# Loading the last row block of an output projection early, through the software DMA queue, in a decode-layer kernel

## The chip, the cores and the metric

The kernel runs on one core of a Trainium2 chip. The metric is device time in microseconds (us). Each run lists the time, the span of the core (first to last instruction that the profile shows) and the mean clock that the throttle granted to the matrix engine (1.0 is full speed).

Names used below: PE is the matrix engine (PEld its weight loads), DVE the vector engine, ACT the scalar engine, POOL the GpSimd engine, SP the engine that issues most transfers. The profile counts 16 DMA engines for a core. A "queue" is where an engine puts its transfers: SP's is q1, ACT's is q10, the software queue that GpSimd fills is q0, and q8 and q14 carry instruction fetches.

## The reference, cut to what matters

```python
# x [8,1,512]; k_cache, v_cache [8,8,4096,128]; wq [512,4096]; wo [4096,512]; bf16
xn = _layernorm(x, axis=-1)
s  = attention(xn, k_cache[..., -1024:, :], v_cache[..., -1024:, :], wq) @ wo   # 32 heads, 8 kv heads
g  = _silu((_gelu(xn @ w_gate) * (xn @ w_up)) @ w_down)                          # width 1792
return x + s * g
```

With 8 tokens, nearly everything is reading weights and cache: 47.6 MB for each execution.

## The kernel before

The kernel streams everything through one SP queue, in the order of use: wq, then keys and values in 1 MB pieces, then the three FFN matrices, then wo. Partition p of a wo tile holds wo rows p*32 to p*32+31. One of these 32 "outer rows" j is a 128 x 512 block of 128 KB: 1 KB on each partition. The output projection is 32 steps of two matmuls, one step for each j, in the order of arrival. The last loads are made smaller and smaller, so that little work is left when the last one lands.

```python
    nc.scalar.dma_start(out=x_sb, in_=x_flat)              # the early copy of x, for the layer norm
    # ... 16 groups of attention; then, with g == NGR, the last loads:
            parts = [(0, 16), (16, 24), (24, 28), (28, 30), (30, 31), (31, 32)]
            wo_t = [load_wo(*q) for q in parts[:2]]        # load_wo issues on nc.sync (the SP queue)
            for t in range(2):
                nc.sync.dma_start(
                    out=x_res[64 * t : 64 * t + B, :], in_=x_flat[:, t * 256 : (t + 1) * 256]
                )
            wo_t += [load_wo(*q) for q in parts[2:]]
    # ...
    for q, (j0, j1) in enumerate(parts):
        for j in range(j0, j1):
            for t in range(2):
                c0 = (j - j0) * D + t * 256
                nc.tensor.matmul(
                    s_ps[64 * t : 64 * t + 64, 0:256],
                    og[:, j : j + 2, :].rearrange("p m b -> p (m b)"),
                    wo_t[q][:, c0 : c0 + 256],
                    start=(j == 0), stop=(j == NOR - 1),
                    tile_position=(0, 64 * t), skip_group_check=True,
                )
    # then out = x_res + s_ps * g_sb on DVE, and two stores
```

The softmax here doesn't subtract the row's maximum and nothing guards it: scores larger than these inputs give would overflow.

## Time and profile before

| | before |
|---|---|
| time, median of 3 runs (range) | 120.79 us (120.64 to 120.92) |
| span of the profiled run | 119.1 us |
| moved by DMA | 47.61 MB, mean 400 GB/s |
| PE, DVE, ACT busy | 73%, 54%, 34% |
| last wo load complete | 115.60 us after the span's start |
| last matmul ends | 115.94 us |

These are lines of the profile page of the kernel before. The rows of digits cut the span into 40 slices of about 3 us; a digit is the busy share or the granted clock of a slice in tenths. The queue lines give packets, MB and the share of 16 engines' time. The last line gives a transfer's size in KB and the median us from issue to landing.

```profile
PE 86.8 (73%) x929; PEld 62.1 (52%) x929; DVE 64.2 (54%) x149; ACT 40.4 (34%) x78; POOL 4.2 (4%) x10
...
PEclk9999999555799999999999999999999965555999
DMA  4999999999999999999999999999999999999940
GB/s 88 432 396 440 418 426 432 418 432 424 418 432 432 432 402 435 429 418 426 429 426 421 429 424 421 429 426 424 429 424 442 426 424 448 420 440 402 405 165 3
...
q1 hardware_dynamic: 6240, 47.46, 95.0%
q8 instruction: 7, 0.11, 0.3%
...
slot<-in_A_k_cache_dram SPq DMA_DIRECT2D x16, 1024.0 KB, 19.7
```

The DMA row stands at 9 from the second slice to the 38th, at a rate that never leaves 396 to 448 GB/s, while no compute engine is that busy. A 1 MB load lands 19.7 us after its issue; such loads complete about 2.45 us apart, so I estimate that it stands in a full queue, about eight deep (19.7 / 2.45). The kernel is bound by its DMA engines.

The end of the chain of waits of the kernel before (start us, length us, what):

```profile
100.62 13.72 DMA slot<-in_A_wo_dram
114.34 0.04 issue
114.38 0.63 PE big L523 x8
...
115.98 0.44 DVE tmp L534
```

And the same place in its timeline (start us, busy us, engine, line, operation, tiles, count, and in brackets the idle time before and what ended it):

```profile
110.60 1.94 PE L523 MATMUL big<-wide_slot,og 128*64 128x256 bf16 x32 [1.60 <-DMA wide_slot<-in_A_wo_dram]
...
114.38 1.56 PE L523 MATMUL big<-slot,og 128*64 128x256 bf16 x16 [0.21 <-DMA slot<-in_A_wo_dram]
...
115.98 0.42 DVE L534 TENSOR_TENSOR tmp<-big,g_sb 128x256 bf16<-128x256 f32 x1 [2.19 <-PE big L523]
```

PE waits for each wo part and ends 0.34 us after the last has landed (115.60 to 115.94). What decides the time is when the last part is complete.

A load shows up to 16 landing events ("posts"), which I read as one from each engine that has a share in it: in this trace the loads of wo over 128 partitions have 16 each, and `x_sb`, in 8 rows, has 8. The load is complete at the last of them: PE's last two matmuls start 0.04 us after it (115.60 to 115.64). The 16 posts of the last part are not in the views above; I list them from the trace (us from the span's start):

```text
113.91 113.95 114.00 114.07 114.09 114.13 | 114.33 114.58 114.85 | 115.24 115.29 115.37 115.39 115.53 115.58 115.60
```

Six engines are done 1.5 us before the last; seven are 1.3 to 1.7 us late. That is the slack that the change is after.

### The profile page before, as it was taken

How to read it: one execution, taken by the hardware profiler on the slowest of the kernel's cores; microseconds unless marked ns; L12 is line 12 of the kernel's file. 1: busy time of each engine (PE TensorE's matmuls, PEld its weight loads, DVE VectorE, ACT ScalarE, POOL GpSimd, SP SyncE). 2: the span in 40 equal slices, each digit the busy share in tenths (PEclk: the TensorE clock that was granted, in tenths of full speed). 3: DMA queues.
4: the chain of work that ended last, by engine and by line, in shares of the span. 5: the costliest groups of instructions: out<-in, count | busy, mean ns of one | idle time of the engine just before them, and what ended most of it. 6: DMA issues, size and time to landing. Idle time of an engine off the chain costs nothing.

```text
span 119.1 us, 2281 instructions
## 1 busy us (share of the span) xinstructions
PE 86.8 (73%) x929; PEld 62.1 (52%) x929; DVE 64.2 (54%) x149; ACT 40.4 (34%) x78; POOL 4.2 (4%) x10
## 2 busy tenths in 40 slices
PE   0013946786999999999998797977979843546680
PEld 0003813563767777686775584755847630133650
DVE  5340644643666866876694664945748424622211
ACT  4000314792443562464354342453424403001100
POOL 7600000000000000000000000000000000000000
PEclk9999999555799999999999999999999965555999
DMA  4999999999999999999999999999999999999940
GB/s 88 432 396 440 418 426 432 418 432 424 418 432 432 432 402 435 429 418 426 429 426 421 429 424 421 429 426 424 429 424 442 426 424 448 420 440 402 405 165 3
DMA packets 6281, 47.61 MB, mean 400 GB/s; under 512 B 728, under 2 KB 1024, under 8 KB 1280
## 3 DMA queue, kind: packets, MB, share of 16 engines
q1 hardware_dynamic: 6240, 47.46, 95.0%
q8 instruction: 7, 0.11, 0.3%
q10 hardware_dynamic: 32, 0.01, 0.0%
q14 instruction: 2, 0.02, 0.0%
HBM read 47.46 MB, written 0.01 MB: 399 GB/s over the span
## 4 chain that ended last, share of the span: by engine, by line
DMA 57%; PE 24%; DVE 10%; ACT 2%; SPq 2%; issue 1%; DVEq 0%
DMA wide_slot<-in_B_w_gate_dram 18%; DMA slot<-in_A_v_cache_dram 16%; PE t_ps L244 12%; DMA slot<-in_A_wo_dram 12%; DMA wide_slot<-in_A_wq_dram 11%; DVE kT L250 8%; PE sc_ps L270 5%; PE o_ps L304 3%; PE big L411 1%; PE big L523 1%; DVE q_all L395 1%; ACT q_all L395 1%; PE big L366 1%; DVE q_sb L379 1%; ACT p L283 1%
## 5 line engine op out<-in xcount | busy, mean ns | idle before, releaser
L250 DVE COPY kT<-t_ps 128x1024 bf16<-128x1024 bf16 x48 | 31.8, 688 | 26.4 <-PE t_ps L244 24.5
L244 PE MATMUL t_ps<-ident_f,slot 128*128 128x128 f32 x256 | 38.5, 301 | 7.8 <-DMA slot<-in_A_k_cache_dram 7.8
L244 PEld LDWEIGHTS t_ps<-ident_f,slot 128*128 128x128 f32 x256 | 31.2, 154 | 18.0 <-issue 7.2
L250 ACT COPY kT<-t_ps 128x1024 bf16<-128x1024 bf16 x16 | 16.2, 1012 | 16.9 <-PE t_ps L244 16.5
L283 ACT ACTIVATE p<-sc_ps 128x512 bf16<-128x512 f32 x16 | 9.6, 597 | 28.4 <-PE sc_ps L270 28.4
L270 PE MATMUL sc_ps<-kT,q_all 128*32 128x512 bf16 x128 | 10.7, 405 | 3.9 <-ACT q_all L395 1.8
L291 DVE STREAM_TRANSPOSE pT<-p 128x512 bf16<-128x512 bf16 x16 | 11.2, 703 | 2.8 <-ACT p L283 2.8
L304 PE MATMUL o_ps<-slot,pT 128*32 128x256 bf16 x256 | 10.1, 278 | 0.0
L324 PE MATMUL a_ps<-selr,o_sb 128*128 128x16 f32 x64 | 9.6, 263 | 0.4 <-ACT o_sb L314 0.3
L324 PEld LDWEIGHTS a_ps<-selr,o_sb 128*128 128x128 f32 x64 | 8.4, 192 | 0.6 <-ACT o_sb L314 0.6
L270 PEld LDWEIGHTS <-q_all 128*32 128x32 bf16 x128 | 3.3, 95 | 7.9 <-issue 3.2
L304 PEld LDWEIGHTS <-pT 128*32 128x32 bf16 x256 | 5.5, 97 | 2.9 <-issue 2.5
L314 ACT COPY o_sb<-o_ps 128x256 f32<-128x256 f32 x16 | 6.0, 378 | 1.3 <-PE o_ps L304 1.3
L260 PE MATMUL sc_ps<-far,hot 4*128 4x512 bf16 x16 | 6.4, 398 | 0.0
L411 PE MATMUL big<-wide_slot,xT 128*32 128x448 bf16 x32 | 3.4, 571 | 3.8 <-DMA wide_slot<-in_B_w_up_dram 2.2
L523 PEld LDWEIGHTS <-og 128*64 128x64 bf16 x64 | 3.5, 109 | 3.7 <-DMA wide_slot<-in_A_wo_dram 2.1
L220 PE MATMUL t_ps<-ident,xhat 32*128 32x32 bf16 x4 | 0.3, 195 | 6.6 <-DVE xhat L210 6.6
L320 PEld LDWEIGHTS a_ps<-ss,ones_f 128*128 128x128 f32 x32 | 4.8, 191 | 0.5 <-DVE oT_all L334 0.3
L453 PE MATMUL big<-wide_slot,hT 128*32 128x256 bf16 x28 | 3.2, 417 | 2.6 <-DMA wide_slot<-in_B_w_down_dram 2.6
L320 PE MATMUL a_ps<-ss,ones_f 128*128 128x16 f32 x32 | 4.9, 229 | 0.0
L333 DVE RECIPROCAL rs<-a_ps 128x16 f32<-128x16 f32 x16 | 4.0, 249 | 1.3 <-PE a_ps L324 1.2
L453 PEld LDWEIGHTS <-hT 128*32 128x32 bf16 x28 | 2.2, 142 | 3.9 <-DVE hT L438 3.4
(64 smaller groups left out, 50.5 us busy)
## 6 DMA issues: line engine op xcount, KB each, us to landing
slot<-in_A_k_cache_dram SPq DMA_DIRECT2D x16, 1024.0 KB, 19.7
slot<-in_A_v_cache_dram SPq DMA_DIRECT2D x16, 1024.0 KB, 19.8
wide_slot<-in_A_wq_dram SPq DMA_DIRECT2D x2, 2048.0 KB, 13.7
wide_slot<-in_A_wo_dram SPq DMA_DIRECT2D x1, 2048.0 KB
wide_slot<-in_B_w_gate_dram SPq DMA_DIRECT2D x1, 1792.0 KB, 21.4
wide_slot<-in_B_w_up_dram SPq DMA_DIRECT2D x1, 1792.0 KB, 23.2
wide_slot<-in_B_w_down_dram SPq DMA_DIRECT2D x1, 1792.0 KB, 25.0
slot<-in_A_wo_dram SPq DMA_DIRECT2D x1, 1024.0 KB
```

The costliest lines, as they stand in the source:

```text
L244: nc.tensor.transpose(kp[:, c * P : (c + 1) * P], kw[:, rp * P : (rp + 1) * P], ident_f)
L250: copy(out=kT_t[g][:, t * 8 * P : (t + 1) * 8 * P], in_=kp.bitcast(BF16))
L260: nc.tensor.matmul(sc, hot.rearrange("n r q -> n (r q)"), far, start=True, stop=False, skip_group_check=True,)
L270: nc.tensor.matmul(sc[32 * t : 32 * t + 32, :], q2_all[:, i, b, e, :, :, :].rearrange("w r n j -> w (r n j)"), kT[:, :, 32 * t : 32 * t + ...
L283: nc.scalar.activation(out=p, in_=sc_t[g], func=ACT.Exp, scale=inv_sqrt_dh, accum_out=acc)
L291: nc.vector.transpose(out=pT, in_=p)
L304: nc.tensor.matmul(o_ps[32 * u : 32 * u + 32, :], pT_t[g][:, m * 32 : (m + 1) * 32], v_t[g][:, m * 256 : (m + 1) * 256], start=(m < 4), st ...
L314: nc.scalar.copy(out=o_sb, in_=o_ps)
L320: nc.tensor.matmul(a_ps[:, 0, :], ones_f, ss_t[g], start=True, stop=True, skip_group_check=True)
L324: nc.tensor.matmul(a_ps[:, 1, :], o_t[g][:, r * Dh : (r + 1) * Dh], selr[:, r, :], start=(r == 0), stop=(r == 1), skip_group_check=True,)
L453: nc.tensor.matmul(f_ps[64 * t : 64 * t + 32, 0:256], hT[:, j, :], wd_t[:, c0 : c0 + 256], start=(j == 0), stop=(j == FR - 1), tile_positi ...
L523: nc.tensor.matmul(s_ps[64 * t : 64 * t + 64, 0:256], og[:, j : j + 2, :].rearrange("p m b -> p (m b)"), wo_t[q][:, c0 : c0 + 256], start= ...
```

## The change

The intent: take outer row 31 of wo (128 KB), and x for the residual, out of the tail, and load them early, through GpSimd's software queue, onto the eight DMA engines that are done first at the end. The source of `wo_last` is written with 8 as its slowest dimension, so that eight engines share it; the x loads, in 8, 4, 2, 2 and 8 rows, are meant to steer which eight engines get it; the last of them, `x_more`, is read by nothing. `x_sb` is cut into four loads of two rows. Because the rows of `wo_last` now lie on other partitions, a second permutation and a second regroup matmul are needed.

```diff
+    wo_last = persist.tile([P, D], BF16, name="wo_last")
+    x_more = persist.tile([B, D // 2], BF16, name="x_more")
+    def load_x_res(t, b0, b1):
+        nc.gpsimd.dma_start(
+            out=x_res[64 * t + b0 : 64 * t + b1, :],
+            in_=x_flat[b0:b1, t * 256 : (t + 1) * 256],
+        )
+    def load_apart():                       # called right after the memset of og
+        load_x_res(0, 0, B)
+        load_x_res(1, 0, 4)
+        load_x_res(1, 4, 6)
+        nc.gpsimd.dma_start(
+            out=wo_last,
+            in_=A_wo.rearrange("(r a j) d -> a r j d", a=B, j=NOR)[:, :, NOR - 1, :],
+        )
+        load_x_res(1, 6, B)
+        nc.gpsimd.dma_start(out=x_more, in_=x_flat[:, 0 : D // 2])
 ...
-    nc.scalar.dma_start(out=x_sb, in_=x_flat)
+    for b0 in range(0, B, 2):
+        nc.scalar.dma_start(out=x_sb[b0 : b0 + 2, :], in_=x_flat[b0 : b0 + 2, :])
 ...
+    perm_last = consts.tile([P, P], BF16, name="perm_last")
+    nc.gpsimd.tensor_copy(
+        out=perm_last.rearrange("p (a r) -> p a r", a=B),
+        in_=perm.rearrange("p (r a) -> p a r", a=B),
+    )
 ... (the one regroup matmul becomes two: perm for rows 0 to 30, perm_last for row 31)
-            parts = [(0, 16), (16, 24), (24, 28), (28, 30), (30, 31), (31, 32)]
-            ... x_res loads on nc.sync
+            parts = [(0, 16), (16, 24), (24, 28), (28, 30), (30, 31)]
 ...
+    rows = [(wo_t[q], j - j0, j) for q, (j0, j1) in enumerate(parts) for j in range(j0, j1)]
+    rows.insert(16, (wo_last, 0, NOR - 1))
```

`(r a j)` with a = 8 puts wo row block r*8 + a on partition a*16 + r.

More of the change, by code (lines that the diff above doesn't have):

```diff
@@ L234 @@
     nc.vector.memset(og, 0.0)
+    load_apart()
     kT_t, p_t, pT_t, ss_t, o_t = {}, {}, {}, {}, {}
@@ L345, in regroup @@
         rg = ps_a.tile([P, B, 32], FP32, name="rg_ps", tag="a")
-        nc.tensor.matmul(
-            rg.rearrange("p b j -> p (b j)"),
-            perm,
-            zt,
-            start=True,
-            stop=True,
-        )
+        for lhs, rhs in (
+            (perm, zt.rearrange("p (b j) -> p b j", b=B)[:, :, 0 : NOR - 1]),
+            (perm_last, zt.rearrange("p (b j) -> p b j", b=B)[:, :, NOR - 1 : NOR]),
+        ):
+            nc.tensor.matmul(
+                rg[:, :, 0 : NOR - 1] if lhs is perm else rg[:, :, NOR - 1 : NOR],
+                lhs,
+                rhs,
+                start=True,
+                stop=True,
+                skip_group_check=True,
+            )
         nc.vector.tensor_copy(
@@ L486 @@
         if g == NGR:
-            parts = [(0, 16), (16, 24), (24, 28), (28, 30), (30, 31), (31, 32)]
-            wo_t = [load_wo(*q) for q in parts[:2]]
-            for t in range(2):
-                nc.sync.dma_start(
-                    out=x_res[64 * t : 64 * t + B, :], in_=x_flat[:, t * 256 : (t + 1) * 256]
-                )
-            wo_t += [load_wo(*q) for q in parts[2:]]
+            parts = [(0, 16), (16, 24), (24, 28), (28, 30), (30, 31)]
+            wo_t = [load_wo(*q) for q in parts]
         if g < NGR:
@@ L518 @@
     s_ps = ps_big.tile([P, 512], FP32, name="big")
-    for q, (j0, j1) in enumerate(parts):
-        for j in range(j0, j1):
-            for t in range(2):
-                c0 = (j - j0) * D + t * 256
-                nc.tensor.matmul(
-                    s_ps[64 * t : 64 * t + 64, 0:256],
-                    og[:, j : j + 2, :].rearrange("p m b -> p (m b)"),
-                    wo_t[q][:, c0 : c0 + 256],
-                    start=(j == 0),
-                    stop=(j == NOR - 1),
-                    tile_position=(0, 64 * t),
-                    skip_group_check=True,
-                )
+    rows = [(wo_t[q], j - j0, j) for q, (j0, j1) in enumerate(parts) for j in range(j0, j1)]
+    rows.insert(16, (wo_last, 0, NOR - 1))
+    for n, (w, at, j) in enumerate(rows):
+        for t in range(2):
+            c0 = at * D + t * 256
+            nc.tensor.matmul(
+                s_ps[64 * t : 64 * t + 64, 0:256],
+                og[:, j : j + 2, :].rearrange("p m b -> p (m b)"),
+                w[:, c0 : c0 + 256],
+                start=(n == 0),
+                stop=(n == NOR - 1),
+                tile_position=(0, 64 * t),
+                skip_group_check=True,
+            )
     tmp = ffn_sb.tile([P, 256], BF16, name="tmp")
```

## The prediction

> **What bounds the kernel now.** The DMA engines. The page's row of slices has them at 9 of 10 in 37 of 40 slices, at 400 GB/s mean; PE is busy 73%, DVE 54%. The issue table has 1 MB loads landing 19.7 us after issue, about eight deep, so engine work, not issue, sets arrival. The chain's jump at 56.3 us from PE to a 19.5 us DMA piece is therefore waiting in a full queue. The end is read from the timeline and the landing events: the last four wo parts land complete at 114.34, 114.97, 115.30 and 115.60 us, and PE only follows (last two matmuls 115.64 to 115.96, then 0.44 + 0.29 us on DVE, then the store).
>
> **Who is last.** A load is complete when its slowest engine has posted. The 16 posts of the last part spread over 113.91 to 115.60 us: six engines together at the start, three at +0.3 to +0.9, seven at +1.3 to +1.7 us. Following packets back to back by engine, these seven are exactly those that each carried one 16 KB instruction fetch (queue 8: 28.0, 41.7, 53.8, 67.1, 77.5, 91.9, 109.3 us). One fetch costs its engine about 1.4 us (its packet 0.93, the next 8 KB packet 0.80 instead of 0.31).[...]
>
> **What the change does.** [...]
>
> - Removed at the end, from every engine: 8 packets of 1 KB, about 43 ns apart, 0.35 us; two x_res rows (0.07 us) from eight engines.
> - Added early to eight quick engines: 16 packets of 1 KB, estimated 0.7 to 0.9 us (the ACT queue's 1 KB packets took 46 ns, the packet after them 10 to 170 ns extra). They remain earlier than +1.3 to +1.7. Two 512 B x rows on the late ones: about 0.06 us.
> - Off the path: GpSimd's issues and perm_last, a second regroup matmul, x_sb landing perhaps 1 to 2 us later (xT is ready at 7.2, first used at 14.2), 0.7 us later early landings, absorbed by the deep queue.
>
> **On the critical path**: the last complete landing moves about 0.3 us earlier; PE, DVE and store after it stay. 120.79 - 0.3 = **120.5 us**, 8 in 10 within **120.15 to 120.95**. Faster by over 2%: 0.01; same: 0.97; slower by over 2%: 0.02.
>
> **Right if**: the last wo part (now row 30) lands complete near 115.3; the seven fetch engines are still last; the eight wo_last engines end 0.7 to 1 us later, so the spread shrinks; a software queue shows 128 packets of 1 KB early.
>
> **Wrong if**: [...]wo_last meets a fetch (about 0.4 us slower instead);[...] the added PE instructions cause an eighth fetch; or the software queue adds fixed time outside the span.

That the eight engines would be quick ones, and the two extra x rows on late ones, was the assumption. 0.35 us less at the end of every engine, and about 0.06 us more on the late ones for two x rows (estimated; a 512 B packet took 27 ns in the trace of the kernel before), come to about 0.3 us, and 120.79 - 0.3 to 120.5 us.

## More of the kernel before

Note the PE clock near the end: four slices at 0.5, then full speed just in time.

For later comparison, the windows of the kernel before (window, its us, then busy us with instruction count of PE, PEld, DVE, ACT and POOL, then the PE clock, the DMA share and GB/s):

```profile
12.00:14.00 2.00, 2.00 (x11) 2.00 (x10) 0.99 (x2) 1.01 (x1) 0.00 (x0) 1.00 0.95 410
14.00:16.00 2.00, 1.62 (x27) 0.73 (x29) 1.04 (x2) 0.00 (x0) 0.00 (x0) 1.00 0.94 397
16.00:18.00 2.00, 0.80 (x18) 0.21 (x9) 1.29 (x2) 0.71 (x2) 0.00 (x0) 1.00 0.98 414
...
44.00:48.00 4.00, 3.95 (x47) 2.97 (x47) 2.90 (x8) 1.82 (x5) 0.00 (x0) 1.00 1.01 426
```

## The result, and the profile after

| | before | after |
|---|---|---|
| time, median of 6 runs (range) | 120.79 us (120.64 to 121.09) | 122.43 us (121.69 to 123.70) |
| span of the profiled run | 119.1 us | 122.0 us (clock 0.858) |
| span of a fast profiled run | 119.1 us | 120.2 us (run again, see below) |

The ratio after to before is 1.0116 (95% interval 1.0084 to 1.0148): slower, but by less than 2%. In this text a ratio is the mean time of one kernel's fast runs over that of the other's fast runs of the same rounds, so it is not quite the ratio of the medians quoted.

The first profile of the kernel after happened to fall on its slowest run. These are lines of its page:

```profile
PEclk9999996555699999999999999999999955555569
...
GB/s 102 415 410 465 323 383 427 427 427 424 427 427 430 422 416 427 430 430 419 427 430 424 422 424 424 427 422 430 427 424 445 418 447 428 431 424 403 298 3 3
```

And from the end of its chain of waits:

```profile
112.24 6.58 PE big L554 x64
```

Two things differ. There is a dip in the GB/s row in the fifth and sixth slice (323 and 383). And the end is bound by PE: its clock stays at half speed to 118.2 us, and the 64 wo matmuls take 6.58 us in one unbroken chain. The second is a matter of this slow run, so it can't explain what the fast runs lose; I ran the same kernel again (label after_again, below). Its page has:

```profile
PEclk9999999557999999999999999999999955556999
...
GB/s 98 427 405 447 337 358 423 428 434 420 425 423 431 425 420 428 420 434 420 428 425 420 431 428 423 425 414 436 431 425 440 421 429 453 408 449 409 397 148 3
...
q1 hardware_dynamic: 6064, 47.32, 94.5%
q0 software_dynamic: 240, 0.14, 0.4%
q8 instruction: 7, 0.11, 0.3%
```

The clock is again full before the end, as in the kernel before. The dip is still there (337 and 358), and the other slices from the second to the 38th stand between 397 and 453, about as before. The windows over the dip, columns as above:

```profile
12.00:14.00 2.00, 2.00 (x11) 2.00 (x10) 0.81 (x2) 0.98 (x1) 0.00 (x0) 1.00 1.02 334
14.00:16.00 2.00, 1.67 (x20) 0.72 (x19) 1.26 (x2) 0.04 (x1) 0.00 (x0) 1.00 0.93 303
16.00:18.00 2.00, 0.72 (x16) 0.36 (x15) 0.00 (x0) 0.00 (x0) 0.00 (x0) 1.00 0.98 398
```

The DMA share is 1.02 and 0.93, as high as before, but the rate falls from 410 and 397 to 334 and 303 GB/s: the engines are not idle, their packets are slower. Over the three windows, (410 - 334 + 397 - 303 + 414 - 398) GB/s x 2 us is 0.37 MB not moved, and at the 426 GB/s of a quiet stretch that is 0.87 us. The timeline at the end of the same run:

```profile
112.09 1.94 PE L554 MATMUL big<-wide_slot,og 128*64 128x256 bf16 x32 [1.67 <-DMA wide_slot<-in_A_wo_dram]
...
114.53 2.48 PE L554 MATMUL big<-slot,og 128*64 128x256 bf16 x30 [0.40 <-DMA slot<-in_A_wo_dram]
...
117.05 0.42 DVE L565 TENSOR_TENSOR tmp<-big,g_sb 128x256 bf16<-128x256 f32 x1 [3.96 <-PE big L554]
```

PE still waits for each part, and all of it is later: the first wo matmul at 112.09 instead of 110.60, the last DVE step at 117.05 instead of 115.98.

Read from the packets and landing events of the two fast traces:

| | before | after_again | difference |
|---|---|---|---|
| slow time of SP's packets, 10 to 18 us, for each engine | 0.00 us | 0.91 us | +0.91 |
| row 30: first engine done | 113.56 | 114.53 | +0.97 |
| row 30: last engine done | 115.30 | 116.67 | +1.37 |
| last load complete (row 31; row 30) | 115.60 | 116.67 | +1.07 |
| last matmul ends | 115.94 | 117.01 | +1.07 |
| span | 119.10 | 120.17 | +1.07 |

"Slow time" is a reading that I use throughout: for every packet of the SP queue, its time less the usual time of its size in a quiet stretch (611 ns for 16 KB, 535 for 14 KB, 309 for 8 KB), summed for each engine, and the mean of 16 engines taken.

So the tail is innocent: PE, DVE and store follow the last landing in both kernels at the same distance. About 0.9 us is lost between 10 and 18 us, while `wo_last` is being loaded, and is never won back: row 30's first engine is still 0.97 us later. In that time half of the 16 KB packets on SP's queue take between 668 and 842 ns instead of 611 (the slowest 907), on all 16 engines, also on the eight that carry none of `wo_last`'s data (in the trace of the kernel after too: at 13.0 and at 14.0 us 16 such packets run at once, and all 16 take over 640 ns).

The rest is in the last two engines. The 16 posts of row 30 in after_again:

```text
114.53 114.63 114.70 | 115.12 115.15 115.17 115.46 | 115.92 116.05 116.06 116.12 116.13 116.15 116.22 | 116.48 116.67
```

An engine can be followed through the trace: its share of a load ends with a packet of 4 bytes, and on an undisturbed engine these lie 2.453 us apart for 1 MB loads, while a fetch on queue 8 puts them off once by 1.41 to 1.53 us. Followed so from 18 us on, the two engines at 116.48 and 116.67 are engines that had carried `wo_last` and then also a fetch on queue 8 (those of 110.9 and 92.6 us; the first of them by exclusion). Engines with a fetch alone are done by 116.22. So of the change of +1.07 us in the last landing, about +0.92 is the slow packets (115.30 to 116.22 for row 30 on engines with a fetch alone), +0.45 is `wo_last` on two engines that were not quick, and -0.30 is the load that is no longer at the end (row 31 landed 0.30 us after row 30).

### The profile page after: what moved, and what is told of

The parts are those of the page before. It is cut to its first block, busy times and chain, and to the rows that moved or that the text cites. A ratio compares the mean times of both kernels' runs of the same rounds, so it can differ in the third digit from the quotient of the medians.

```text
span 122.0 us, 2295 instructions
## 1 busy us (share of the span) xinstructions
PE 90.6 (74%) x930; PEld 64.9 (53%) x930; DVE 64.2 (53%) x149; ACT 40.4 (33%) x78; POOL 7.9 (6%) x17
## 4 chain that ended last, share of the span: by engine, by line
DMA 56%; PE 24%; DVE 11%; ACT 4%; issue 1%; SPq 1%; DVEq 0%
DMA wide_slot<-in_B_w_gate_dram 18%; DMA slot<-in_A_v_cache_dram 16%; DMA wide_slot<-in_A_wq_dram 12%; DMA wide_slot<-in_A_wo_dram 10%; PE t_ps L274 9%; DVE kT L280 7%; PE big L554 5%; PE sc_ps L300 4%; PE o_ps L334 3%; ACT q_all L430 2%; DVE q_all L430 2%; PE big L446 1%; ACT L313 1%; PE t_ps L422 1%; PE big L401 1%
## 5 line engine op out<-in xcount | busy, mean ns | idle before, releaser
L554 PEld LDWEIGHTS <-og 128*64 128x64 bf16 x64 | 5.3, 169 | 3.8 <-DMA wide_slot<-in_A_wo_dram 2.8
L554 PE MATMUL big<-wide_slot,og 128*64 128x256 bf16 x32 | 3.6, 421 | 2.3 <-DMA wide_slot<-in_A_wo_dram 2.3
```

Source lines behind the costliest of these rows:

```text
L554: nc.tensor.matmul(s_ps[64 * t : 64 * t + 64, 0:256], og[:, j : j + 2, :].rearrange("p m b -> p (m b)"), w[:, c0 : c0 + 256], start=(n == ...
```

## The experiments

The theories at the start were: (A) the transfers of the software queue slow everything, because the software queue as such is costly (its descriptors, its extra small packets); (B) what costs is how `wo_last` is spread: eight engines for all 128 partitions, so that they write partitions that other engines are filling at the same time; (C) the strided source is slow to read (row blocks 256 KB apart); (D) the engines chosen are not the quick ones.

### after_again: the kernel after, once more

No edit.

> The changed kernel, unedited, to see it in its fast state and how its times and clocks scatter. My theory A (a DMA loss): all 16 engines lose about 1 us between 12 and 16 us, in every run, so the last wo landing stays about 1 us later than in the kernel before. My theory B (a PE clock loss): the low-clock window (0.5) that covers the end of the profiled slow run is only partly there in a fast run; then the last matmul follows the last landing by under 1 us instead of 2.2 us. Expected time 121.7 to 122.6 us, span 120.0 to 120.9. A rival, that all of the loss is the clock, expects a last landing within 0.3 us of the 115.6 us of before.

Measured: 121.94 us median (121.63 to 122.68, 4 runs), ratio 1.0111 (1.0071 to 1.0151). The fast profile is the one shown above. The loss is real. Theory D is right in part: two of the eight `wo_last` engines also got a fetch on queue 8 in this trace, and one did in the slow trace of the same kernel and one in that of sw_flat. These are the last to post each time, at 116.67 against 116.22 for the others, 116.64 against 116.09, and 116.69 against 116.30, so this costs 0.4 to 0.55 us. It leaves the dip unexplained.

### sw_flat: a source within one block, everything else the same (a wrong result on purpose)

```diff
-            in_=A_wo.rearrange("(r a j) d -> a r j d", a=B, j=NOR)[:, :, NOR - 1, :],
+            in_=A_wo[0:P, :].rearrange("(r a) d -> a r d", a=B),
```

> Wrong result on purpose: wo_last is read from 128 neighbouring rows of wo (rows 8 KB apart inside an outer row) instead of rows 256 KB apart; the same queue, engines, bytes and descriptors. If the source's large stride slows the engines, the 16 KB packets beside it return from 670-860 ns to about 611 ns and the time falls by about 1 us, to near 121.0. If the software queue or the 8-engine placement does it, packets stay at 670-860 ns and the time stays at 121.7-122.6.

Measured: 122.24 us (121.93 to 122.48), ratio 1.0122 (1.0103 to 1.0141). The windows of the dip:

```profile
12.00:14.00 2.00, 2.00 (x12) 2.00 (x11) 0.91 (x2) 1.01 (x1) 0.00 (x0) 1.00 1.05 359
14.00:16.00 2.00, 1.58 (x19) 0.63 (x18) 1.17 (x2) 0.00 (x0) 0.00 (x0) 1.00 0.93 305
```

The source is now one block of 128 KB, in which the rows of one of its eight parts lie 8 KB apart instead of 256 KB. The dip stays (359 and 305 GB/s), slow time 0.89 us between 12 and 18 us, and the last landing is 116.69 against 116.67. The source's stride is not the cause: theory C falls. (The values of row 31 are wrong here; the comparison with the reference still passed its tolerance.)

### hw_same: the same transfers from ACT's hardware queue

```diff
-        nc.gpsimd.dma_start(          # all of load_x_res, wo_last and x_more
+        nc.scalar.dma_start(
```

> The same six early loads from the ACT hardware queue instead of GpSimd's software queue[...]. If the software queue itself slows all engines, the 16 KB packets beside it stay near 611 ns and about 1 us comes back[...], time about 121.1 plus any clock loss. If the source's stride or eight engines are to blame, the dip stays and the time is 121.7 or more.

(The 121.1 us holds 0.35 us for a term: that two of the engines would also carry a fetch. No trace showed which engines they would be.)

Measured: 121.96 us (121.66 to 122.39), ratio 1.0103 (1.0079 to 1.0127). The transfers come a little later, and so does the dip; the windows show it moved two us on (323 and 373 GB/s at a DMA share of 0.90 and 1.05):

```profile
16.00:18.00 2.00, 0.80 (x17) 0.21 (x10) 1.29 (x2) 0.69 (x2) 0.00 (x0) 1.00 0.90 323
18.00:20.00 2.00, 1.48 (x17) 0.93 (x17) 0.72 (x1) 1.06 (x2) 0.00 (x0) 1.00 1.05 373
```

Slow time between 16 and 20 us is 0.51 us, less than 0.91, but the last landing is 116.99. The engines here need not be the same as with the software queue, and the posts spread over 2.9 us. The software queue is not needed for the dip, nor for the loss. Theory A falls as the main cause. That the software queue alone adds nothing is shown by sw_16 below; why the slow time is 0.51 here and 0.91 there stays open.

### sw_x_only: only the x loads stay on the software queue

Row 31 goes back to the end of SP's queue; the four x loads, `x_more` and the split `x_sb` stay.

```diff
-        nc.gpsimd.dma_start(out=wo_last, in_=A_wo.rearrange("(r a j) d -> a r j d", ...)[:, :, NOR - 1, :])
-            parts = [(0, 16), (16, 24), (24, 28), (28, 30), (30, 31)]
+            parts = [(0, 16), (16, 24), (24, 28), (28, 30), (30, 31), (31, 32)]
-    rows.insert(16, (wo_last, 0, NOR - 1))
```

> The software queue carries the five x loads alone[...]; wo row 31 is back at the tail on the SP queue; x in four loads and the two regroup matmuls stay. If wo_last's own transfer makes the dip (stride or software descriptors of a large transfer), there is no dip and the time is within 0.3 us of before, 120.6 to 121.1. If merely using the software queue, or the late x (8.4 us instead of 4.4), costs the time, it stays above 121.5.

Measured: 121.18 us (121.09 to 121.59), ratio 1.0042 (1.0024 to 1.0061). No slow time, last landing 115.61 and last matmul 115.95, as in the kernel before. The small rest, 0.27 us of span (119.37 against 119.10), comes after the stores, at the program's end: SP passes the last of its closing waits 0.33 us after the last store has landed, in the kernel before 0.08 us. So the x loads do not make the dip, and `wo_last` does.

### sw_16: the software queue, natural order, 16 engines

The same 128 KB at the same time from the same queue, but partition p gets its own row, so that the transfer is laid out as SP's full-width loads are (16 posts each in the kernel before).

```diff
-            in_=A_wo.rearrange("(r a j) d -> a r j d", a=B, j=NOR)[:, :, NOR - 1, :],
+            in_=wo_rows[:, (NOR - 1) * D : NOR * D],
 ...
-            (perm_last, zt...[:, :, NOR - 1 : NOR])
+            (perm, zt...[:, :, NOR - 1 : NOR])
```

> As the changed kernel, but wo_last's source is left in its natural order, 128 outer rows, so that the software transfer uses all 16 engines (perm instead of perm_last). Same queue, time, bytes and 1 KB rows. If it is the placement on 8 engines[...] that slows all engines, the 16 KB packets beside it stay within 5% of 611 ns, the excess per engine over 10 to 20 us falls from 0.9 us to under 0.2 us, and the last landing comes back to about 115.7 us (time about 121.1, with 0.3 us of extra end as in the x-only run). If any small-row transfer beside the big one slows them, the excess stays at 0.6 to 0.9 us and the last landing at 116.4 or later.

Measured: 120.83 us (120.69 to 121.41), ratio 1.0013 (0.9984 to 1.0042). The windows of the place where the dip was:

```profile
12.00:14.00 2.00, 2.00 (x12) 2.00 (x11) 0.73 (x2) 0.84 (x1) 0.00 (x0) 1.00 1.00 424
14.00:16.00 2.00, 2.00 (x16) 0.88 (x18) 1.38 (x2) 0.17 (x1) 0.00 (x0) 1.00 0.93 388
```

No slow time (0.00 us), last landing 115.47, span 118.97. This one run acquits the software queue, the early loading and the changed PE program: the spread is left. (One thing goes with the spread: in the kernel after, the software queue also has 32 packets of 16 bytes (9 to 14 ns each in the trace of the kernel after), presumably on the eight engines without data, and sw_16 has none of these. hw_same and hw_k4 have the dip without any, so they are not needed for it.) It also shows why sw_16 wins nothing: each engine has the same 8 KB of row 31 as before, only earlier, so that the late engines stay as late.

### tail_k4: only the spread, at the end of SP's queue

The kernel before, with row 31 as its last load still, but with 4 as the slowest dimension: four engines (four posts, below), hoped to be quick ones, with a quarter of the 128 rows each.

```diff
-            wo_t += [load_wo(*q) for q in parts[2:]]
+            wo_t += [load_wo(*q) for q in parts[2:-1]]
+            wo_last = slot()
+            nc.sync.dma_start(
+                out=wo_last[:, 0:D],
+                in_=A_wo.rearrange("(r a j) d -> a r j d", a=4, j=NOR)[:, :, NOR - 1, :],
+            )
+            wo_t += [wo_last]
 ... (perm_last with a=4, and the second regroup matmul)
```

> The kernel before, with wo row 31 still last on the SP queue but taken with four outer rows[...]. If the balance idea holds and no other engine is slowed, the last landing comes 0.2 to 0.35 us earlier than 115.60 and the time is 120.4 to 120.6. If a transfer on few engines slows all 16, the late engines lose it again: last landing 115.6 or later, time 120.8 to 121.5.

Measured: 121.34 us (121.03 to 121.42), ratio 1.0041 (1.0022 to 1.0060). The last landing is not earlier but 0.13 us later, 115.73: row 30 is complete at 115.43, and row 31 posts on its four engines at

```text
114.86 114.95 115.44 115.73
```

So two of the four were not quick; own_k4 shows why this can be. The time lies where the expectation put the rival, that a transfer on few engines slows all 16, but the packets show little of it here: no slow time, and of the 1 and 2 KB packets at the end 11 took longer than usual (up to 58 instead of 46 ns, and 105 instead of 84). PE ends at 116.17, 0.44 us after the landing, with its clock at half speed to 114.6 us; all four runs have granted clocks of 0.881 to 0.886.

### hw_k4 and hw_16: the spread alone, in the middle of the kernel

Row 31 early, by ACT's queue at the fifth attention group; hw_k4 with 4 as the slowest dimension, as in tail_k4 (four posts there), hw_16 in natural order, laid out as SP's full-width loads (16 posts each in the kernel before). The rest is the same in both.

```diff
+        if g == 4:
+            nc.scalar.dma_start(
+                out=wo_last,
+                in_=A_wo.rearrange("(r a j) d -> a r j d", a=4, j=NOR)[:, :, NOR - 1, :],  # hw_k4
+                in_=wo_rows[:, (NOR - 1) * D : NOR * D],                                   # hw_16
+            )
```

> wo row 31 alone taken early (group 4, near 40 us) by the ACT hardware queue with four outer rows[...]; x as before. Balance without the software queue: if no other engine is slowed, last landing about 115.25 and time about 120.5. If a transfer on few engines slows all 16, an excess of 0.4 to 0.9 us per engine shows near 40 us, last landing 115.7 to 116.2.

> Control of hw_k4: the same early load by the ACT hardware queue in its natural order, on all 16 engines. Placement theory: no excess near 40 us, and as the bytes of every engine are those of before, last landing 115.6 within 0.1 us, time 120.7 to 120.9. Small-row theory: an excess of 0.4 us or more, last landing 116 or later.

Measured, hw_k4: 124.43 us (124.21 to 124.91), ratio 1.0307 (1.0281 to 1.0334), last landing 119.28. Measured, hw_16: 121.06 us (120.68 to 121.86), ratio 1.0012 (0.9976 to 1.0048), last landing 115.70. The two kernels differ only in how the 128 rows are laid over engines and partitions, and by nearly 3% in time.

In hw_k4 two costs add up. One line of the waits of its SP queue (us in total, times, longest us), and three of its windows:

```profile
SPq L101 <- DMA wo_last<-in_A_wo_dram: 16.7, 1, 16.7
```

```profile
48.00:52.00 4.00, 3.95 (x51) 3.03 (x47) 2.90 (x8) 1.82 (x5) 0.00 (x0) 1.00 1.01 370
52.00:56.00 4.00, 3.08 (x34) 2.22 (x27) 2.31 (x6) 1.67 (x4) 0.00 (x0) 1.00 0.87 320
56.00:60.00 4.00, 3.83 (x46) 2.72 (x44) 3.06 (x7) 1.36 (x3) 0.00 (x0) 1.00 0.71 256
```

First, slow packets: 370 GB/s at a DMA share of 1.01, slow time 1.01 us for each engine between 43.7 and 55.3. Second, and new, an empty queue: SP waited 16.7 us once for `wo_last` and issued nothing from 38.8 to 56.15, so that by 56 to 60 us the DMA share falls to 0.71 and the rate to 256 GB/s. SP does not use `wo_last`; the wait stands before the load of a later piece of keys or values (L101). The reason is a semaphore that both queues' transfers share: in the trace `wo_last` signals its landing on semaphore 108, and the load that SP issues at 56.15 signals on 108 too, right after the last landing of `wo_last` at 56.09. In hw_16 SP also waited for it, 9.8 us, but the queue did not run empty, and slow time was 0.03 us. The window with the load in it, in hw_16:

```profile
44.00:48.00 4.00, 3.95 (x48) 2.91 (x47) 3.05 (x7) 1.91 (x4) 0.00 (x0) 1.00 1.01 417
```

hw_16 teaches a second thing. Its four runs are 121.86, 120.68, 121.43 and 120.68 us, with granted clocks of 0.882, 0.914, 0.886 and 0.914. The page and then the timeline of its profiled run (the one of 121.86) show where that comes from:

```profile
PEclk9999999955589999999999999999999995555578
```

```profile
111.07 3.62 PE L541 MATMUL big<-wide_slot,og 128*64 128x256 bf16 x32 [1.58 <-DMA wide_slot<-in_A_wo_dram]
...
114.70 2.27 PE L541 MATMUL big<-slot,og 128*64 128x256 bf16 x30
```

The first 32 wo matmuls take 3.62 us instead of 1.94, and the next begin without a wait for their data. PE, at half clock to 115.6 us, is behind the DMA, and ends at 116.97, 1.27 us after the last landing. While PE waits for the FFN's matrices and for wo its clock is at half, and it is full again only some time into the last stage: in the slow profile of the kernel after it is at half from 97.7 to 118.2 us, in after_again from 96.5 to 110.2. What halves it and what brings it back, no run here shows. Where the full clock comes back differs from trace to trace, and costs 0.93 us here (PE ends 1.27 us after the last landing instead of 0.34). The four runs differ by 1.2 us (121.86 against 120.68), but only the slowest was traced, so how much of that is the clock is not shown; the mean granted clock alone does not tell (the kernel before took 120.67 us at 0.885 and 120.64 at 0.913).

### dead_own and dead_other: the same load on other partitions

So far two things have come together: fewer engines, and engines that write partitions which other engines fill in SP's loads. In a 1 MB load of SP an engine has 8 of the 128 partitions, if a packet fills one (eight packets of 8 KB, 309 ns each, in the 2.453 us of a load); with the 128 spread over eight or four engines, it has 16 or 32, so at least half of them are some other engine's in any of SP's loads. This pair of runs keeps the number of engines and changes the partitions. Here is the kernel before with 64 KB of dead data loaded by ACT's queue at the fifth group, in two transfers of 32 partitions. Both have 8 as the slowest dimension, so eight engines should share each transfer (eight posts for the 8 rows of `x_sb` in the kernel before). dead_own writes partitions 0 to 63, dead_other 64 to 127. Which of these the same engines also fill in SP's loads is not shown, since the profile names neither the engine nor the partition of a packet; "own" and "other" were the assumption. Only the destination (and with it the source rows) differs.

```diff
+        if g == 4:
+            for p0 in (0, 32):        # dead_own;   (64, 96) in dead_other
+                nc.scalar.dma_start(
+                    out=dead[p0 : p0 + 32, :],
+                    in_=A_wo[p0 * NOR : (p0 + 32) * NOR, :].rearrange(
+                        "(r a j) d -> a r j d", a=8, j=NOR
+                    )[:, :, NOR - 1, :],
+                )
```

> The kernel before plus a load that nothing reads (64 KB: wo row 31 of partitions 0 to 63, two transfers of 32 partitions with eight outer rows, ACT hardware queue, near 40 us).[...] Own-partition theory (an engine slows others only when it writes partitions that another engine fills at that time): no excess of the big packets, under 0.1 us per engine. Concentration theory (few engines with many small rows slow all): an excess of 0.25 us or more per engine, the same as in the twin run. Time:[...] 120.9 to 121.2.

> The twin: the same load[...], same sizes, but of partitions 64 to 127[...]. Own-partition theory: an excess of 0.25 us or more per engine, time at least 0.2 us above the twin. Concentration theory: no difference between the two.

Measured, dead_own: 121.20 us (121.06 to 121.36), ratio 1.0027 (0.9993 to 1.0060); slow time 0.00; last landing 115.88. Measured, dead_other: 121.87 us median, ratio 1.0077 (1.0045 to 1.0109) from three fast runs. Its profiled run took 147.96 us at a clock of 0.576, so that its trace says nothing about this.

### dead_other_again: for a fast profile of dead_other

> The twin of the own-partition run once more, because its profile fell in a slow state (clock 0.5 from start to end). Own-partition theory: excess of the big packets 0.2 us or more per engine within the 3 us of the transfer, last landing at least 0.25 us after that of the twin (115.88); concentration theory: both as in the twin.

Measured: 121.66 and 121.85 us, ratio 1.0071 (1.0039 to 1.0102), last landing 116.35. The same window of dead_own, then of dead_other_again:

```profile
44.00:48.00 4.00, 3.95 (x48) 2.91 (x47) 2.90 (x7) 1.82 (x5) 0.00 (x0) 1.00 1.01 423
```

```profile
44.00:48.00 4.00, 3.95 (x48) 2.90 (x47) 2.89 (x8) 1.82 (x5) 0.00 (x0) 1.00 1.02 390
```

With the same bytes, the same queue, the same slowest dimension and the same time, the rate is 423 GB/s with partitions 0 to 63, which is near the 426 of the kernel before, and 390 with 64 to 127; slow time is 0.00 against 0.31 us, and the last landing differs by 0.47 us. The packets say the same: in dead_own all 64 packets of dead data take 46 ns and the 8 KB packets beside them 309; in dead_other_again they take up to 72 and up to 384. So fewer engines are not enough for the slowing; which partitions they write makes the difference. That it is whether they are their own is the author's reading, not shown. (The source rows change along with the partitions. sw_flat makes them an unlikely cause, but these very rows were not tested apart.)

### own_k4: the change on partitions that showed no slowing

If that is so, row 31 can be given to quick engines without the dip. Four pieces of 32 rows, one for each group, with 4 as the slowest dimension, each put on partitions 0 to 15 and 32 to 47, which are among those of dead_own. The four pieces lie side by side in the free dimension; the output projection has 35 steps instead of 32, and one slot less in the ring.

```diff
+    wo_last = persist.tile([P, NQ * D], BF16, name="wo_last")      # NQ = 4
+    def load_last(m):                                              # at g = 4 + m
+        for h in range(2):
+            p0 = 32 * m + 16 * h
+            nc.scalar.dma_start(
+                out=wo_last[32 * h : 32 * h + 16, m * D : (m + 1) * D],
+                in_=A_wo[p0 * NOR : (p0 + 16) * NOR, :].rearrange(
+                    "(r a j) d -> a r j d", a=4, j=NOR)[:, :, NOR - 1, :],
+            )
```

> The intent of the change without its cost, if the own-partition theory holds: row 31 of wo is taken early by the ACT hardware queue in four pieces of 32 rows, each into partitions 0-15 and 32-47[...]; each piece has its own permutation matrix and its own two matmuls (35 row steps instead of 32), and the ring has 13 slots instead of 14. Expected: no excess near 40 to 55 us (under 0.1 us per engine), last landing 115.2 to 115.35 instead of 115.60, time about 120.45 (ratio 0.997 to 0.998) if the low PE clock does not reach the tail. Rival: any transfer on four engines slows all 16, then the excess is above 0.5 us as in the four-row run and the time above 121.5.[...]

Measured: 121.91 us (121.48 to 122.91, 6 runs), ratio 1.0100 (1.0060 to 1.0140), last landing 116.60. The dip is gone: no slow time while the pieces land (44 to 54 us). The time is not. A line of the waits of its SP queue, and a window:

```profile
SPq L102 <- DMA wo_last<-in_A_wo_dram: 7.7, 4, 4.6
```

```profile
56.00:60.00 4.00, 3.44 (x44) 2.53 (x33) 2.44 (x7) 1.80 (x4) 0.00 (x0) 1.00 0.97 383
```

SP waited for the pieces four times, and the queue ran low at 56 to 60 us (383 GB/s; some 0.3 us). And two of the four engines were not quick: each carried, besides 32 KB of row 31, a fetch on queue 14 (at 41.0 and 54.6 us). Read from the packets, the fetch costs its engine about 0.85 us (309 ns for itself, and the packet behind it 838 to 861 ns instead of 309; in the kernel before the two fetches of queue 14 cost 0.83 and 0.54), and the 32 KB 1.38 us. Their sum, 2.2 us, is more than the 1.3 to 1.7 us by which the slowest engines trail. They were the last.

### own_k6_sp: six engines, SP's own queue

The same by SP's queue, so that no second queue can hold it up: six pieces, one for each of the groups 3 to 8, with 6, 6, 6, 6, 4 and 4 as slowest dimension, meant for six engines, on partitions 0 to 23 and 32 to 55. That would be 16 to 24 KB for each engine, by own_k4's 1.38 us for 32 KB an estimated 0.7 to 1.05 us; with a fetch on queue 14 (0.85 us) 1.55 to 1.9, about as late as the late ones (1.7).

```diff
+    pieces = [(0, 6, 0), (24, 6, 0), (48, 6, 1), (72, 6, 1), (96, 4, 2), (112, 4, 2)]
+    def load_last(n):                 # at g = 3 + n
+        p0, a, m = pieces[n]
+        h = 32 * (n % 2)
+        nc.sync.dma_start(
+            out=wo_last[h : h + 4 * a, m * D : (m + 1) * D],
+            in_=A_wo[p0 * NOR : (p0 + 4 * a) * NOR, :].rearrange(
+                "(r a j) d -> a r j d", a=a, j=NOR)[:, :, NOR - 1, :],
+        )
```

> own_k4 without its two faults: the six pieces of row 31 go through the SP queue in turn, one per group, so no load waits for a transfer that ACT issues late[...]. Expected: no excess of the big packets beside the pieces (under 0.1 us per engine) and no dip of the DMA row near 56 us; last landing 115.25 to 115.5 instead of 115.60; time within 0.3 us of before, 120.4 to 121.0 depending on the PE clock in the tail. If the last landing is 115.7 or later, the balance idea itself is wrong, not only its placement.

Measured: 122.06 us (121.51 to 122.78, 6 runs), ratio 1.0114 (1.0084 to 1.0145). The GB/s row of its page:

```profile
GB/s 93 422 409 463 403 431 433 420 422 425 428 433 417 425 420 431 428 422 412 436 421 435 417 422 431 425 425 431 425 425 441 434 420 439 446 431 390 363 40 5
```

No dip, no slow time, no wait. Fourteen engines have posted by 115.22 us, 0.38 us before the 115.60 of the kernel before, as hoped for. But two trail, at +1.92 and +2.10 us after the first (1.04 for the moved bytes, 0.85 for a fetch on queue 14), and the load is complete at 115.65. Then PE, with 68 matmuls and a half clock to 114.3 us, ends at 116.52 instead of 115.94, and the program's end is 0.58 us longer: SP passes the last of its closing waits 0.71 us after the last store has landed, instead of 0.08. Why was not traced further. The gain is there in the fourteen engines, and the two late ones, the slow clock and the longer end more than eat it.

### All runs together

| label | what | median us | ratio to before | slow time, us | last landing |
|---|---|---|---|---|---|
| after_again | the change | 121.94 | 1.0111 | 0.91 | 116.67 |
| sw_flat | source within one block | 122.24 | 1.0122 | 0.89 | 116.69 |
| hw_same | ACT's queue | 121.96 | 1.0103 | 0.51 | 116.99 |
| sw_x_only | without wo_last | 121.18 | 1.0042 | none | 115.61 |
| sw_16 | natural order, 16 engines | 120.83 | 1.0013 | 0.00 | 115.47 |
| tail_k4 | 4 engines, at the end | 121.34 | 1.0041 | none | 115.73 |
| hw_k4 | 4 engines, mid-kernel | 124.43 | 1.0307 | 1.01 | 119.28 |
| hw_16 | 16 engines, mid-kernel | 121.06 | 1.0012 | 0.03 | 115.70 |
| dead_own | +64 KB, partitions 0 to 63 | 121.20 | 1.0027 | 0.00 | 115.88 |
| dead_other_again | +64 KB, partitions 64 to 127 | 121.75 | 1.0071 | 0.31 | 116.35 |
| own_k4 | row 31, partitions among 0 to 63, 4 engines | 121.91 | 1.0100 | 0.34 (empty queue) | 116.60 |
| own_k6_sp | the same, 6 engines, SP | 122.06 | 1.0114 | none | 115.65 |

No version is faster than the kernel before; sw_16, hw_16 and dead_own equal it within their intervals.

## Why the prediction was wrong, point by point

**The direction and size of the time: wrong.** Predicted 120.5 us (120.15 to 120.95); measured 122.43, and 121.94 when run again. The chance of 0.97 for "within 2%" pointed at the right class, since 1.0116 is within 2%, but the range does not hold the time.

**What bounds the kernel, and who is last: right.** The tail follows the last landing: last landing, last matmul and span all moved by 1.07 us between the two fast traces.

**Where the transfers go: right in number, wrong in place.** In the trace, `wo_last` went to eight engines, as expected (32 data packets in four rounds of eight). But they were not the engines without a fetch: two of the eight also carried one on queue 8, and two others those on queue 14. The prediction had named this under "Wrong if" ("wo_last meets a fetch (about 0.4 us slower instead)"), and the size fits the 0.45 us above. There were still seven fetches on queue 8. All 16 engines post for `wo_last` all the same: it has 16 landing events in the trace of the kernel after, and the software queue has 16 more packets of 4 bytes than in sw_x_only (152 against 136). The detail of the packets was wrong: 32 of 4096 bytes, at 159 to 229 ns each in after_again, not 128 of 1 KB. Undisturbed (159 ns in sw_16), one such packet takes nearly what the forecast had for four rows (4 x 46 ns).

**x later: right that it is harmless.** `x_sb` landed at about 8.4 us instead of 4.4, later than the "1 to 2 us" forecast; the first matmul of the query projection came at 14.50 instead of 14.24, and the deep queue of loads did not notice.

**The step that failed**: "Added early to eight quick engines: 16 packets of 1 KB, estimated 0.7 to 0.9 us [...] They remain earlier". It failed in two places. First, "quick": two of the eight had a fetch as well, and they ended last, 0.45 us after the others. Second, and larger, it counts each DMA engine's work as its own account. But the runs show a cost for all 16 engines, which no entry of the sum had: `wo_last`, laid over eight engines in this way, slows everyone's packets, by 0.91 us for each engine, three times the 0.3 us to be gained. That `wo_last` is responsible is shown by sw_x_only; that its source stride is not, by sw_flat; that the software queue is not, by hw_same and sw_16; that fewer engines are not enough and that it matters which partitions they write, by dead_own (0.00) against dead_other_again (0.31). I had thought of the number of engines and not asked where they write. That the engines slow each other by writing partitions which others are filling is my reading of these runs; they show that it depends on the partitions, and not why.

**Which engines are quick: not known beforehand.** Engines were called quick because they carried no fetch on queue 8 in the trace of the kernel before. There one such fetch of 16 KB took 931 ns on its engine, and the 8 KB packet behind it 805 ns instead of 309: about 1.4 us. In the kernel after, two of the eight got one; in the slow trace of the same kernel it was one, so the meeting of transfers and fetches differs between executions. In own_k4 and own_k6_sp two engines carried a fetch on queue 14, which costs 0.85 us there and which the prediction's sum does not have, and these were the last to post. Whether the transfers or the fetches fell elsewhere than assumed is open, since the profile does not name the engines. Because the kernel after has one load less at its end, the net loss in landing is 1.07 and not 1.37 us.

**A term not in the sum: the PE clock.** "PE, DVE and store after it stay" held in the fast profile (0.34 us from landing to last matmul in both kernels), and not in the slow one, in which the half clock lasted to 118.2 us and PE ended 2.16 us after the last landing. The runs of the kernel after scatter from 121.69 to 123.70, those of before from 120.64 to 121.09. The clock can be part of the scatter (it is in the one trace of hw_16); that the change made it likelier was not tested.

**"The software queue adds fixed time outside the span"** was named as a risk. It is small: time less span is 1.74 us in after_again, about 1.65 before. **"An eighth fetch"** did not come.

What stays open besides: whether the slow packets at 56 us in own_k4 come only from the refilled queue; and how the slowing grows with the number of such partitions (0.31 us for 64 KB in dead_other_again, 0.91 for 128 KB in after_again, are two points of different make).

## What to carry to other kernels

In this kernel, bound by its DMA engines, moving bytes from late to early engines could win no more than the spread of the landing events, 1.7 us, of which 0.3 was in reach; and it cost at least that wherever the small transfer slowed the packets beside it (0.31 to 1.01 us for each engine). In the pair that differs in the partitions written (and the source rows with them) they made the difference: 0.00 us on partitions 0 to 63 (dead_own), 0.31 on 64 to 127 (dead_other_again). Test such a transfer in the middle of the stream by itself, with dead data, and read the rate beside the DMA share: 390 GB/s at a share of 1.02 meant slower packets for all (dead_other_again), 256 GB/s at 0.71 an empty queue, because the issuing queue had waited 16.7 us for the small transfer (hw_k4). Check which engines the instruction fetches of every queue burden (about 1.4 us for one on queue 8, 0.54 to 0.85 on queue 14), and in more than one execution, before calling an engine quick, and look at the clock at the end before believing half a us (it cost 0.93 us in the trace of hw_16). None of the versions tried here won.
